# Weight staging as single jobs given out by an account of engine times, and x kept as seven fp32 pieces

## The chip, the core and the metric

One core of one Trainium2 chip runs the kernel. Time is device time in microseconds, from runs of the whole program. PE is TensorE (matmuls, into PSUM), DVE is VectorE, ACT is ScalarE, POOL is GpSimd, SP is the engine that only issues DMAs here; each works through its own queue in order. ACT issues a few DMAs too.

## The reference

Attention without softmax, a norm, and two gated networks, one after the other:

```python
kv = np.einsum('bhsd,bhse->bhde', k, v)            # 8 batches, 8 heads, 576 tokens, 64 wide
out = np.einsum('bhsd,bhde->bhse', q, kv)
rms = np.sqrt(np.mean(out * out, axis=-1, keepdims=True) + 1e-06)
x = (out / rms * g_norm)                           # then 4608 tokens x 512
gate = 1.0 / (1.0 + np.exp(-(x @ w_gate)))         # first network, 512 -> 1536 -> 512
x = gate * (x @ w_val) @ w_out
g = x @ w_gate2                                    # second network, same sizes
silu = g * (1.0 / (1.0 + np.exp(-g)))
y = silu * (x @ w_val2) @ w_out2
```

The weights arrive as float64.

## The kernel before

**Tiling.** The 4608 tokens are nine blocks j of 512. Each network's 1536 columns are twelve slices of 128, and a phase (the list `PH`) walks all nine blocks with six of them: phases 0 and 1 are the first network, 2 and 3 the second. A phase's half of the output goes to DRAM (`pd`) and is added to in the next one. A matmul in full fp32 precision is three in the fast format fp32r: every operand is split into a high part (a copy that rounds, on ACT) and a low part (source minus high part, on DVE or POOL), and low x high, high x low and high x high are summed in one PSUM bank.

**Seven products.** Phase 0 multiplies plainly (`gv_plain`, units of one slice). In phases 1 to 3 a unit is two slices and runs Winograd's form of the 2x2 block product (`gv_win`): seven products of 12 matmuls in place of eight, in the order 11, T2, T1, T3, 21, 22, T4 of x. For that x comes in seven pieces of 128 x 512, namely three quarters of the block and four differences of quarters, each with high and low part, 14 in all; the weights come in seven pieces too. Behind a unit's seven products stand the output products of the unit before (`parts_of(tail)`, `finish`).

**x of the first network.** The attention leaves x in DRAM (`xd`). In phase 1 `x_steps` loads four quarters per block into `xl` buffers, forms the differences and both parts, and writes them into one of two sets of x tiles, one to the right (`x`), one to the left (in `arena`), in turn.

**x of the second network.** When a block of phase 1 is done, `comp_steps` splits its seven pieces and stores the 14 parts to DRAM (`xc`), through two places of `spare` in turn, and for the last block through two `raw` buffers (`xz`). In phases 2 and 3 there is one set of x tiles: `x_load` stands behind each product of a block's last unit and loads the next block's piece, both parts, 512 KB, into the place that this product was the last to read.

**Weights.** `rounded` makes fp32 out of a float64 chunk by six steps (`o1` on ACT, `o3` to `o6` on DVE, `o7` on DVE or POOL). Phase 0's own weights are rounded directly into place (`put_direct`). For the later phases `stage` and `stage_pair` load a chunk into `raw`, round it, form the sums, split them and store them to DRAM (`wd`); `place`, `place_most` and `place_seven` load them from there shortly before use. 72 chunks of 128 x 512 are rounded in all.

**What sets the order.** The program is written in the order of PE's work; ACT, DVE and POOL keep the order of writing nearly everywhere, while SP's DMAs are ordered by a scheduler from their readiness. Between products `tick` advances the count `now` and lets queues of thunks (`att`, `xq`, `kq`, `wq`, `pq`, `rq`) run at a pace that meets their due times; `budget` limits how many DVE and POOL steps one tick may emit. Phase 1's weights are in `pq`, those of phases 2 and 3 in `rq`, as fixed lists of steps:

```python
    def pace(self, dt, pairs=False):
        rate = dt * max(((i + 1) / max(1, z[0] - now[0]) for i, z in enumerate(self.items[self.at:])), default=0.0)
        self.credit = min(self.credit + rate, 1.0 + rate)
        n = int(self.credit)
        self.credit -= n
        self.run(n, True, pairs)
```

## Time and profile before

| | us |
|---|---|
| median of 3 runs (lowest, highest) | 1775.51 (1774.17, 1776.54) |
| the profiled execution | 1774.87 |
| its span, from the first to the last instruction | 1773.1 |

Granted TensorE clock over the span: 0.995 of full speed. Busy time by stretch, in us, and the busy share of the 16 DMA engines:

| stretch | about | PE | DVE | ACT | POOL | DMA |
|---|---|---|---|---|---|---|
| 100 to 545 | phase 0 | 444.37 | 245.83 | 162.15 | 205.99 | 0.63 |
| 545 to 958 | phase 1 | 412.63 | 336.84 | 177.44 | 260.86 | 0.64 |
| 958 to 1367 | phase 2 | 402.32 | 276.17 | 154.45 | 217.50 | 0.57 |
| 1367 to 1773 | phase 3 | 401.37 | 232.34 | 126.03 | 170.14 | 0.43 |

Matmuls overlap one another and their ends are modelled, so a busy PE can still lose time between them; how far apart equal pieces of its work start tells more than its busy share.

### The profile page before, as it was taken

The numbers are of one execution on the slowest core, as the hardware profiler recorded it, in microseconds if no ns is written. First come the engines' busy times: TensorE is split into PE (matmuls) and PEld (weight loads), VectorE is DVE, ScalarE is ACT, GpSimd is POOL, SyncE is SP. The second block draws the span as 40 slices with busy tenths as digits, with TensorE's granted clock in tenths as the row PEclk, the third lists the DMA queues.
The fourth block names the chain that finished last, engine by engine and source line by source line (L and its number), as shares of the span: only waits on it lengthen the run. The fifth ranks groups of instructions, "written<-read, shape, count | busy, mean of one in ns | idle before, by whom it ended". The sixth has DMA issues, their size and how long they took to land.

```text
span 1773.1 us, 33796 instructions
## 1 busy us (share of the span) xinstructions
PE 1745.6 (98%) x12844; PEld 1629.4 (92%) x12844; DVE 1160.1 (65%) x1853; ACT 677.6 (38%) x1472; POOL 898.2 (51%) x991
## 2 busy tenths in 40 slices
PE   7899999999999999999999999999999999999998
PEld 6788888888889999999999999999999999999998
DVE  5766556554455888988875666767775555555555
ACT  4654233333343444444443333433333333333332
POOL 1654456531254576767662455556563344444444
PEclk8999999999999999999999999999999999999999
DMA  9968796457457455565679834444459743343432
GB/s 290 276 166 229 225 229 158 123 153 244 143 178 281 160 181 194 191 220 176 201 272 353 295 118 165 175 174 164 170 185 331 245 132 131 131 132 131 132 131 72
DMA packets 282467, 339.39 MB, mean 191 GB/s; under 512 B 96192, under 2 KB 205376, under 8 KB 282048
## 3 DMA queue, kind: packets, MB, share of 16 engines
q1 hardware_dynamic: 267136, 324.11, 56.4%
q10 hardware_dynamic: 15168, 13.11, 2.5%
q8 instruction: 101, 1.65, 0.4%
q14 instruction: 62, 0.51, 0.1%
HBM read 217.09 MB, written 120.06 MB: 190 GB/s over the span
## 4 chain that ended last, share of the span: by engine, by line
PE 91%; DMA 4%; POOL 2%; DVE 1%; issue 1%; ACT 0%; SPq 0%; DVEq 0%; POOLq 0%; ACTq 0%
PE gv L795 42%; PE gv L717 16%; PE o L928 14%; PE o L907 8%; PE o L893 8%; PE ops L222 1%; DMA vm<-in_v_dram 1%; PE kvps L172 1%; DMA x<-xc 1%; DMA raw<-in_moe_w_out_dram 1%; DMA xc<-xz 0%; PE xTp L269 0%; DMA pl<-pd 0%; DMA xd<-xT 0%; POOL he L837 0%
## 5 line engine op out<-in xcount | busy, mean ns | idle before, releaser
L795 PE MATMUL gv<-x,wgv 128*128 128x256 f32 x5796 | 694.3, 280 | 7.0 <-DMA x<-xc 3.2
L795 PEld LDWEIGHTS gv<-x,wgv 128*128 128x128 f32 x5796 | 685.9, 188 | 10.3 <-ACT u L803 2.3
L717 PE MATMUL gv<-x,wgv 128*128 128x512 f32 x1296 | 315.4, 394 | 3.1 <-ACT x L276 2.3
L717 PEld LDWEIGHTS gv<-x,wgv 128*128 128x128 f32 x1296 | 241.4, 189 | 53.7 <-ACT x L276 2.8
L342 DVE TENSOR_TENSOR u<-u,gv 128x512 f32<-128x512 f32 x162 | 110.1, 680 | 83.0 <-PE gv L795 79.2
L893 PE MATMUL o<-h,wo 128*128 128x512 f32 x648 | 161.4, 393 | 0.0
L893 PEld LDWEIGHTS o<-h,wo 128*128 128x128 f32 x648 | 120.1, 188 | 24.2 <-issue 0.3
L768 ACT ACTIVATE w<-v 128x256 f32<-128x256 f32 x81 | 33.9, 418 | 235.4 <-DVE v L342 224.8
L795 PEld LDWEIGHTS gv<-arena,wgv 128*128 128x128 f32 x1008 | 119.5, 188 | 1.3 <-DVE v L342 0.2
L795 PE MATMUL gv<-arena,wgv 128*128 128x256 f32 x1008 | 119.9, 279 | 0.0
L725 DVE TENSOR_TENSOR sg<-sg,gv 128x512 f32<-128x512 f32 x54 | 36.9, 683 | 102.1 <-PE gv L717 99.5
L907 PE MATMUL o<-h,arena 128*128 128x512 f32 x432 | 101.5, 390 | 0.0
L837 POOL TENSOR_TENSOR spare<-w,spare 128x256 fp32r<-128x256 f32 x54 | 42.6, 788 | 112.6 <-ACT spare L836 112.5
L421 POOL TENSOR_TENSOR u<-u,s 128x512 f32<-128x512 f32 x36 | 49.6, 1377 | 97.9 <-DVE s L418 85.8
L837 POOL TENSOR_TENSOR he<-w,he 128x256 fp32r<-128x256 f32 x54 | 41.8, 775 | 109.1 <-ACT he L836 109.1
L907 PEld LDWEIGHTS o<-h,arena 128*128 128x128 f32 x432 | 79.8, 188 | 15.9
L407 DVE TENSOR_SCALAR u<-u 128x512 uint32<-128x512 uint32 x72 | 48.1, 668 | 65.3 <-ACT u L403 65.0
L342 DVE TENSOR_TENSOR v<-g,gv 128x512 f32<-128x512 f32 x81 | 55.7, 687 | 53.0 <-PE gv L795 32.9
L928 PE MATMUL o<-arena,h 128*128 128x256 f32 x636 | 83.0, 279 | 0.0
L837 POOL TENSOR_TENSOR spare<-g,spare 128x256 fp32r<-128x256 f32 x54 | 49.3, 932 | 66.3 <-ACT spare L836 66.3
L928 PE MATMUL o<-arena,he 128*128 128x256 f32 x648 | 81.5, 279 | 0.0
L928 PE MATMUL o<-arena,spare 128*128 128x256 f32 x648 | 81.5, 279 | 0.0
(155 smaller groups left out, 3030.8 us busy)
## 6 DMA issues: line engine op xcount, KB each, us to landing
x<-xc SPq DMA_DIRECT2D x126, 512.0 KB, 5.3
wgv<-wd SPq DMA_DIRECT2D x72, 448.0 KB, 7.5
xc<-spare SPq DMA_DIRECT2D x112, 256.0 KB, 3.3
pl<-pd SPq DMA_DIRECT2D x80, 256.0 KB, 4.3
wd<-raw SPq DMA_DIRECT2D x72, 256.0 KB, 2.3
raw<-in_moe_w_gate_dram SPq DMA_DIRECT2D x24, 512.0 KB, 5.2
raw<-in_moe_w_val_dram SPq DMA_DIRECT2D x24, 512.0 KB, 4.4
raw<-in_moe_w_out_dram SPq DMA_DIRECT2D x24, 512.0 KB, 4.7
```

The source lines that it names most:

```text
L172: nc.tensor.matmul(kvps[b][e * D:(e + 1) * D, hp, :D], lt, rt, start=(r == hp == 0), stop=(r == R and hp == NP - 1), skip_group_check=True)
L342: nc.vector.tensor_tensor(out=out, in0=a, in1=b, op=ALU.add)
L407: nc.vector.tensor_scalar(ub, ub, 3, None, op0=ALU.logical_shift_left)
L421: (E_O7 if eng is not nc.vector else eng).tensor_tensor(out=st["u"], in0=st["u"], in1=st["s"], op=ALU.add)
L717: nc.tensor.matmul(ps, w[:, e, a, kk, :], x[b][:, kk, :], start=(n == 0), stop=(n == 3 * KD - 1))
L725: nc.vector.tensor_tensor(out=sg, in0=sg, in1=bank[1], op=ALU.mult)
L768: nc.scalar.activation(o, t[:, 0], AF.Silu if f else AF.Sigmoid)
L795: nc.tensor.matmul(ps[:, e], w[:, l, kk], xs[x_at(r)[0]][:, x_at(r)[1], kk], start=(fresh and e == n == kk == 0), stop=(not more and e == ...
L837: nc.gpsimd.tensor_tensor(out=hs[z][:, 1], in0=x, in1=hs[z][:, 0].bitcast(F32), op=ALU.subtract)
L893: nc.tensor.matmul(ps, l, r, start=(fresh and t == 0), stop=(last and t == 2))
L907: nc.tensor.matmul(ps, l, r, start=(fresh and e == t == 0), stop=(last and e == 1 and t == 2))
L928: nc.tensor.matmul(ps[:, t], h[:, r, cs], w[:, Ax[a] + 7 * l], start=(start and t == n_ == 0), stop=(stop and t == 1 and n_ == 2), skip_gr ...
```

## The change

Three things change, and the matmuls stay.

**Jobs.** `stage` and `stage_pair` go. `group_jobs` cuts the staging of a pair of slices into single jobs: a load, each step of a rounding, each sum, copy, subtraction and store. A job names the engines that may do it with a time for each, and the buffers it touches. An account holds the time of PE's work so far (`clock`, advanced by `passed` behind each product) and when each engine will be free (`free`, advanced by `use` beside every instruction of the kernel and by `moved` for DMAs). `pump` gives out the job that can start soonest on an engine whose backlog stays under `HORIZON`, as long as more jobs remain than `LINE_` allows at this point. Where DVE or POOL can do a job, the account chooses.

**x in seven fp32 pieces.** `seven_steps` makes the four differences of the first network's x in phase 0 (for blocks 0 to 2 from a second reading) and stores them (`x7`, three quarters stay in `xd`); `comp_steps` stores the second network's seven pieces as they are, the differences made in place behind the store of what they overwrite. `x_load` now serves phases 1 to 3 and loads one fp32 piece, 256 KB, into the place of the low part; `run_splits` then puts a copy (high part) at 4.2 us and a subtraction in place (low part) at 5.2 us behind the load, by the account. One set of x tiles is left.

**Buffers.** The left set of x tiles goes; in its room stands `stage`, with buffers for two more groups of jobs in phase 1 (sides B and C), and later `arena`, which holds the output weights of phases 2 and 3 together with the new `wob`. In phase 0 there are buffers in the room of the x tiles (side R, `aside`) and of the attention (side T). Staging now ends in phase 1 (`ASIDE_END`).

```diff
+    def use(e, share=1.0):
+        free[e] = max(free[e], clock[0]) + share * WORK[e]
+    def sooner(k):
+        c = clock[0]
+        e = "V" if max(free["V"], c) + 0.85 <= max(free["G"], c) + 1.4 + FAVOR[k] else "G"
+        use(e)
+        return e
+    def moved(mb):
+        free["D"] = max(free["D"], clock[0]) + mb / 0.39
+    def passed(n, cols):
+        clock[0] += n * (0.117 if cols == HB else 0.228)
...
-        late["arena"] = shifted(late["L"], 11 * KB, F32R, ARENA_AT, "arena")
+        late["wob"] = shifted(late["L"], 4 * KB, F32R, ARENA_AT, "wob")
         late["spare"] = late["L"].tile([P, 8, HB], F32R, name="spare")
+        late["stage"] = shifted(late["L"], 7 * KB, U32, W7_AT, "stage", "ar")
...
+    def pump():
...
+        while len(jobs) > floor:
+            held_keys, best = set(), None
+            for n, z in enumerate(jobs[:WINDOW]):
+                keys = z.keys | old_of(z) | ({(side_of(z), z.new[0])} if z.new else set())
+                if not keys & held_keys:
+                    r = max((ready.get(k, 0.0) for k in keys), default=0.0)
+                    for e, d in z.does.items():
...
+                        t = max(clock[0], free[e])
+                        start = max(t, r)
+                        d = shared(e, d, start)
+                        if start <= t + BUBBLE[e] and start + d <= clock[0] + HORIZON[e] * short - soon.get(e, 0.0):
+                            best = min(best or (9e9,), (round(max(start - t, 0.0) / STEP) + (start + d) / 100 * (len(z.does) > 1), n, e, start))
+                held_keys |= keys
+            if not best:
+                return
+            emit(jobs[best[1]], best[2], best[3])
...
     def x_load(ph, j, b):
         k, i = x_at(b)
-        t = x_tiles(ph, j)[k][:, i:i + 2].rearrange("p c k a -> p (c k a)").bitcast(F32)
-        nc.sync.dma_start(out=t, in_=xc[j][:, 2 * b * DM:2 * (b + 1) * DM])
+        h, l = [x_tiles(ph, j)[k][:, i + e] for e in range(2)]
+        if PH[ph][0]:
+            nc.sync.dma_start(out=l.rearrange("p k a -> p (k a)").bitcast(F32), in_=xc[j][:, b * DM:(b + 1) * DM])
+        elif b > 2:
+            nc.sync.dma_start(out=l.rearrange("p k a -> p (k a)").bitcast(F32), in_=x7[j][:, (b - 3) * DM:(b - 2) * DM])
...
+        def hi():
+            nc.scalar.activation(h, l.bitcast(F32), AF.Copy)
+            use("A")
+        def lo():
+            ENG[sooner(0)].tensor_tensor(out=l, in0=l.bitcast(F32), in1=h.bitcast(F32), op=ALU.subtract)
+        splits.extend(((clock[0] + LANDED, hi), (clock[0] + LANDED + 1.0, lo)))
...
+    def run_splits():
+        while splits and splits[0][0] <= clock[0]:
+            splits.pop(0)[1]()
...
-        return [H(0, 0, 0), W(0, 0, 0), D((0, 0), (0, 1), (0, 0)), H(1, 1, 2), W(1, 1, 2), D((0, 1), (1, 1), (0, 1)), H(0, 0, 3), W(0, 0, 3, po), nop, D((0, 0), (1, 1), (0, 0)),
-                H(0, 1, 5), W(0, 1, 5, po), nop, H(1, 0, 1), W(1, 0, 1), D((1, 0), (1, 0), (0, 0)), H(0, 0, 4), W(0, 0, 4, po), nop, H(1, 0, 6), W(1, 0, 6, po)]
+            return lambda: ENG[sooner(1)].tensor_tensor(out=st[o], in0=st[a], in1=st[b], op=ALU.subtract)
+        return [store(0, 0, 0), store(1, 1, 2), store(1, 0, 1), nop, nop, D((0, 0), (0, 1), (0, 0)), nop, store(0, 0, 3), D((0, 1), (1, 1), (0, 1)), nop, store(0, 1, 5),
+                nop, nop, D((0, 0), (1, 1), (0, 0)), nop, store(0, 0, 4), D((1, 0), (1, 0), (0, 0)), nop, store(1, 0, 6)]
...
+    def between():
+        run_splits()
+        if "L" in late and now[0] >= tick_of(*ASIDE_END):
+            drain("B", "C")
+        if wq.at >= n_direct[0] and not -5 <= now[0] - tick_of(1, 0, 0) < 13 and not HOLD[0] <= now[0] - tick_of(2, 0, 0) < HOLD[1]:
+            pump()
...
     def tick(dt=1.0, room=9, pool=1):
         now[0] += dt
+        run_splits()
...
-        if not first and not -5 <= now[0] - tick_of(1, 0, 0) < 13:
-            if pq.at < len(pq.items):
-                pq.pace(dt)
-            else:
-                rq.pace(dt, HOLD <= now[0] - tick_of(2, 0, 0) < 42)
+        between()
```

**ACT in the first unit of phase 2's second block.** Here `he`, `hl`, `v` and `w` belong to the unit before, `xz` is a split piece of the second network's last block, and `u<-gv` is the copy of the new unit's first product. Before:

```order
L768 ACTIVATE v<-g 128x256
L836 ACTIVATE he<-w 128x256
L682 ACTIVATE xz<-pl 128x512
L768 ACTIVATE w<-u 128x256
L682 ACTIVATE xz<-pl 128x512
L836 ACTIVATE he<-g 128x256 x2
L836 ACTIVATE he<-w 128x256
L803 ACTIVATE u<-gv 128x512
L836 ACTIVATE hl<-v 128x256
```

The same place in the changed kernel, where `x_4990` to `x_4992` are the three tiles of x:

```order
L970 ACTIVATE v<-g 128x256
L1044 ACTIVATE he<-w 128x256
L819 ACTIVATE x_4991<-x_4991 128x512
L819 ACTIVATE x_4992<-x_4992 128x512
L970 ACTIVATE w<-u 128x256
L819 ACTIVATE x_4990<-x_4990 128x512 x2
L1044 ACTIVATE he<-g 128x256 x2
L1044 ACTIVATE he<-w 128x256
L1010 ACTIVATE u<-gv 128x512
```

The two `xz` copies left their places, and copies of loaded x pieces stand there.

**SP at the change to the last block of phase 2** (`wd` is staged weights, `xc` the second network's x, `pd` the half outputs, `wgv` phase 3's weights). Before:

```order
L605 DMA x_9024<-xc_10108 128x1024
L605 DMA x_9025<-xc_10108 128x1024
L469 DMA wd_11_465<-raw 128x256
L605 DMA x_9025<-xc_10108 128x1024
L605 DMA x_9026<-xc_10108 128x1024
L469 DMA wd_11_465<-raw 128x512 x2
L605 DMA x_9024<-xc_10108 128x1024 x2
L469 DMA wd_11_465<-raw 128x512
L469 DMA wd_11_465<-s 128x512
L469 DMA wd_11_465<-u 128x512
L469 DMA wd_11_465<-s 128x512
L605 DMA x_9026<-xc_10108 128x1024
```

After:

```order
L1182 DMA pd_6_13730<-yg 128x2x256
L1182 DMA pd_6_13730<-yu 128x2x256
L810 DMA x_4990<-xc_10125 128x512
L810 DMA x_4991<-xc_10125 128x512 x2
L810 DMA x_4992<-xc_10125 128x512
L810 DMA x_4990<-xc_10125 128x512 x2
L810 DMA x_4992<-xc_10125 128x512
L773 DMA wgv_6_14444<-wd_6_460 128x896 x3
```

The stores of staged weights have left the stretch, and each x load has half the columns.

**SP at the turn from phase 2 to phase 3** (`arena<-wd` is phase 3's output weights). Before:

```order
L572 DMA wgv_8_14850<-wd_8_462 128x896 x4
L605 DMA x_9024<-xc_5910 128x1024
L605 DMA x_9025<-xc_5910 128x1024 x2
L572 DMA wgv_9_14871<-wd_9_463 128x896 x4
L605 DMA x_9026<-xc_5910 128x1024
L594 DMA arena<-wd_7_461 128x256 x2
L594 DMA arena<-wd_7_461 128x768 x2
L605 DMA x_9024<-xc_5910 128x1024 x2
L605 DMA x_9026<-xc_5910 128x1024
```

After:

```order
L773 DMA wgv_8_14696<-wd_8_462 128x896 x4
L810 DMA x_4990<-xc_5994 128x512
L810 DMA x_4991<-xc_5994 128x512
L773 DMA wgv_9_14717<-wd_9_463 128x896
L810 DMA x_4991<-xc_5994 128x512
L773 DMA wgv_9_14717<-wd_9_463 128x896 x3
L810 DMA x_4992<-xc_5994 128x512
L798 DMA arena<-wd_7_461 128x256 x2
L798 DMA arena<-wd_7_461 128x768 x2
L810 DMA x_4990<-xc_5994 128x512 x2
L810 DMA x_4992<-xc_5994 128x512
```

The weights stand around x as before, one of them now between the second and the third piece, and x's loads are half as large.

## Rows read from the trace of the kernel before

**Rows 1.** The page's first part: busy time, share of the span, instructions.

```profile
PE 1745.6 (98%) x12844; PEld 1629.4 (92%) x12844; DVE 1160.1 (65%) x1853; ACT 677.6 (38%) x1472; POOL 898.2 (51%) x991
```

**Rows 2.** Stretches: length, busy PE, PEld, DVE, ACT, POOL (instructions), clock, DMA, GB/s.

```profile
100.00:545.00 445.00, 444.37 (x2375) 370.02 (x2373) 245.83 (x370) 162.15 (x291) 205.99 (x264) 1.00 0.63 178
545.00:958.00 413.00, 412.63 (x2915) 386.07 (x2915) 336.84 (x485) 177.44 (x356) 260.86 (x200) 1.00 0.64 221
...
545.00:560.00 15.00, 15.00 (x111) 14.18 (x111) 4.96 (x10) 4.96 (x10) 0.00 (x0) 1.00 0.98 355
```

**Rows 3.** The chain in order of time, phase 1: start us, us, what.

```profile
574.82 9.80 PE gv L795 x84
...
605.37 9.80 PE gv L795 x84
...
666.46 9.80 PE gv L795 x84
...
942.66 9.80 PE gv L795 x84
```

**Rows 4.** The chain, phase 2 and the first block of phase 3.

```profile
973.20 5.62 PE gv L795 x48
...
1013.53 8.48 PE o L928 x72
...
1057.83 8.40 PE o L928 x72
1066.23 9.80 PE gv L795 x84
...
1101.96 8.40 PE o L928 x72
...
1234.34 8.47 PE o L928 x72
...
1278.99 8.54 PE o L928 x72
...
1324.72 8.40 PE o L928 x72
...
1372.64 8.40 PE o L928 x72
```

**Rows 5.** Timeline, phase 2's second block: start us, us, what [idle before, releaser].

```profile
1005.32 0.63 ACT L682 ACTIVATE xz<-pl 128x512 fp32r<-128x512 f32 x1 [4.22 <-DMA xc<-xz]
...
1006.77 0.57 ACT L803 ACTIVATE u<-gv 128x512 f32<-128x512 f32 x1
...
1007.40 3.07 PE L795 MATMUL gv<-x,wgv 128*128 128x256 f32 x24 [1.21 <-ACT u L803]
```

**Rows 6.** The chain: two loads of x, from issue to landing.

```profile
1315.32 7.62 DMA x<-xc
...
1357.94 7.87 DMA x<-xc
```

**Rows 7.** Timeline, SP at the change to phase 2's last block.

```profile
1314.67 0.32 SPq L469 DMA_DIRECT2D wd<-s  x1
```

**Rows 8.** Splits of x by line, whole span: duration ns min/median/max, first, last start.

```profile
L656 ACT ACTIVATE x<-xl x35: 614/618/635, 507.3 to 906.4; 128x512 fp32r<-128x512 f32 x35
...
L659 POOL TENSOR_TENSOR x<-xl,x x20: 1281/1302/1755, 520.4 to 909.2; 128x512 fp32r<-128x512 f32 x20
...
L659 DVE TENSOR_TENSOR x<-xl,x x15: 682/841/1828, 510.7 to 903.1; 128x512 fp32r<-128x512 f32 x15
```

**Rows 9.** X loads of 512 KB between 1380 and 1700 us.

```profile
DMA to landing us min/median/max: 3.4/5.0/6.8
```

**Rows 10.** DMA issues, 1400 to 1700 us: KB each, median us to landing.

```profile
pl<-pd SPq DMA_DIRECT2D x32, 256.0 KB, 3.5
```

**Rows 11.** DMA issues, 1340 to 1375 us.

```profile
x<-xc SPq DMA_DIRECT2D x7, 512.0 KB, 7.9
```

**Rows 12.** Timeline, the first unit of phase 3.

```profile
1365.94 4.59 PE L795 MATMUL gv<-x,wgv 128*128 128x256 f32 x24 [1.98 <-DMA x<-xc]
```

More of the change, by code (lines that the diff above doesn't have):

```diff
@@ new lines, in sides, with side_of, drain @@
+    def sides():
+        if "L" in late:
+            return ("B", "C") if now[0] < tick_of(*ASIDE_TO) else ()
+        return ("R",) if "R" in late and clock[0] < ASIDE[0] else ()
+    def side_of(z):
+        if z.group.side is None:
+            for k in sides():
+                if not any(y.group.side == k for y in jobs):
+                    return k
+            return "A"
+        return z.group.side
+    def drain(*which):
+        while any(z.group.side in which for z in jobs):
+            z = next(z for z in jobs if z.group.side in which)
+            emit(z, next(iter(z.does)), clock[0])
@@ new lines, in shared, with emit @@
+    def shared(e, d, start):
+        if e == "V":
+            return d + min(SHARE[0], max(0.0, free["G"] - start))
+        if e == "G":
+            return d + min(SHARE[1], max(0.0, free["V"] - start))
+        return d
+    def emit(z, e, start):
+        keys = z.keys | old_of(z)
+        jobs.remove(z)
+        z.group.side = side_of(z)
+        if z.new:
+            rings.setdefault((z.group.side, z.new[0]), []).append(z.new[1])
+        if e == "D":
+            z.f()
+            moved(z.does["D"])
+            end = max(clock[0] + 2.0, free["D"]) + LATE
+        else:
+            (z.f(e) if len(z.does) > 1 else z.f())
+            start = max(start, clock[0])
+            end = start + shared(e, z.does[e], start)
+            free[e] = max(free[e], end)
+            end += 0.1
+        for k in keys:
+            ready[k] = end
@@ new lines, in T_tile, with begin_small @@
+    def T_tile(t, n):
+        x = aside["T"][t if t != "u" else f"u{n}"]
+        return x.bitcast(U32).rearrange("p (a b) -> p a b", b=2) if t == "raw" else x
+    def begin_small():
+        if "R" in late or wq.at < n_direct[0] or any(z.group.side == "T" for z in jobs) or now[0] >= tick_of(*T_TO):
+            return
+        fresh = []
+        for z in jobs:
+            if z.group.side is None and z.group not in fresh:
+                fresh.append(z.group)
+        if len(fresh) < 2:
+            return
+        if "T" not in aside:
+            t = {"raw": at.tile([P, DM, 2], U32, tag="raw", name="raw").rearrange("p a b -> p (a b)"), "u0": at.tile([P, DM], F32, tag="u", name="u")}
+            t["u1"], t["s"], t["sg0"], t["sg1"] = [wk.tile([P, NB], F32, tag="sn", bufs=4, name=n) for n in ("us", "ss", "sg", "sg")]
+            aside["T"] = t
+        g = fresh[1]
+        k = next(i for i, z in enumerate(jobs) if z.group is g)
+        n = sum(z.group is g for z in jobs)
+        jobs[k:k + n] = group_jobs(*g.of, True)
@@ L680, in run, with S, store @@
+                moved(0.25)
+            return run
+        def S(i, n):
+            def run():
+                hi, lo = [t[:, 2 * i:2 * i + 2, n * HB:(n + 1) * HB] for t in x_tiles(0, j)]
+                split(hi, lo, st[i, n])
+            return run if use_ else nop
+        def D(o, a, b):
+            return lambda: sub(st[o], st[a], st[b])
+        def store(i, n, o):
             def run():
-                z[o] = buf()
-                nc.scalar.activation(z[o][:, :2], st[i, n], AF.Copy)
@@ L739, in h_places @@
             hw["n"] = 0
-        if p == 2 and first:
-            while not rq.whole():
-                rq.run(1)
-            hw["far"] = [wk.tile([P, 2, HB], F32R, tag=t, name="hl") for t in "usu"]
-        elif p == 2 and len(hw["L"]) == 2:
+        if p == 2 and len(hw["L"]) == 2:
             hw["L"].append([wk.tile([P, 2, HB], F32R, tag="xl", bufs=3, name="hl") for _ in range(3)])
@@ L1123, in evac @@
             if i == 1:
-                ring = [0]
-                def buf():
-                    if j == NBLK - 1:
-                        return wk.tile([P, 4, HB], F32R, tag="raw", name="xz")
-                    ring[0] ^= 4
-                    return late["spare"][:, ring[0]:ring[0] + 4]
-                while j == NBLK - 1 and not rq.whole():
-                    rq.run(1)
-                th = comp_steps(j, {divmod(z, 2): part.pop((ph, j, z)) for z in range(4)}, buf)
+                th = comp_steps(j, {divmod(z, 2): part.pop((ph, j, z)) for z in range(4)})
                 for k, z in enumerate(th):
@@ L1358, in attention_two_ffn @@
                 first = (ph, j) == (1, 0)
[L1359 to L1361 removed]
+                if not queued and (i > 1 or j > 0) and ph == 0 and (nxt[0] == 0 or "R" in late):
                     queued = True
```

446 lines of the change are left out of this document (277 added, 169 removed).

## The prediction

> **What bounds the kernel now.** I read the page first. The matmuls cover 98% of the span [rows 1], so the time is the list of matmuls plus what TensorE loses between them. The change leaves the list alone: on PE's queue both programs hold 12336 matmuls of the same shapes, in the same order but for 88 of them in phase 0, where whole groups change place. So I only ask where TensorE stands still. The stretches by phase come next: from 100 us on the granted clock is 1.00, the upper of TensorE's two levels (2.4 GHz), and phase 0 and phase 1 are covered to within 0.6 us of PE time [rows 2]. "Covered" hides short holes, since a matmul's end is modelled, so I took the chain of waits as a clock: the same piece of work stands there once a unit or once a block, and a distance that is too long is a loss.
>
> Phase 1: four undisturbed units take 666.46 - 605.37 = 61.09, or 15.27 each. The 24 units from 574.82 to 942.66 take 367.84 where 366.54 are due: 1.30 lost [rows 3].
>
> Phases 2 and 3: the last output products of a block (72 matmuls) recur every 1101.96 - 1057.83 = 44.13 us where nothing disturbs. Before that, 1013.53 to 1057.83 is 44.30 (0.17 lost); 1234.34 to 1278.99 is 44.65 (0.52); 1278.99 to 1324.72 is 45.73 (1.60); 1324.72 to 1372.64, in which phase 2 turns into phase 3, is 47.92 (3.79). From a block's second unit to those products it is 1101.96 - 1066.23 = 35.73; across the turn from phase 1 to phase 2 it is 1013.53 - 973.20 = 40.33 (4.60) [rows 4]. After 1372.64 nothing is lost.
>
> The sum is 1.30 + 4.60 + 0.17 + 0.52 + 1.60 + 3.79 = 12.0 us. That is nearly all that a change of staging can win. What is lost in the first 100 us belongs to the attention and the first weights; the orders are the same there on all queues until about 145 us.
>
> **The change part by part.**
>
> *x of the second network, compressed (turn from phase 1 to phase 2).* Before, the last block's x is cut into high and low halves in two `xz` buffers, and ScalarE may write the next one only after a store has landed. It stands in order: at 1005.32 it has idled 4.22 us for such a store, and behind it wait the `he` copies and the copy `u<-gv` that PE needs at 1007.40 [rows 5]. The changed kernel has no `xz`: the fp32 piece is stored as it is, and ScalarE's row there holds only copies of x pieces whose loads left a unit earlier. What goes is 4.60. What is late next: VectorE or GpSimd now overwrite a piece only after its store has landed, which holds up the next stores but nobody on PE's path, since those pieces are read a phase later. Between 0 and 4.60 left; I take 0.4, near the low end, because the row names the cause and it is gone.
>
> *No staging in phase 2.* Of the 72 roundings of a weight chunk, 44 stand before phase 1, 16 in it and 12 in phase 2. In the changed order it is 47, 25 and 0. So SP's queue in phase 2 holds no weight stores between the x loads. The last x load of a block leaves only at 1315.32, when the weight stores ahead of it on the queue have left, the last of them at 1314.67; it lands 7.62 us later, and PE waits [rows 6, 7]. The losses 0.17, 0.52 and 1.60 should go: left between 0 and 2.29, taken 0.3.
>
> *x as seven fp32 pieces, split in place.* Each of the 126 loads shrinks from 512 to 256 KB, and 63 stores of 256 KB go as well. Added are, per block of phases 1 to 3, seven copies on ScalarE (0.62 us each) and seven subtractions, 155 of 189 of them on VectorE (0.68 alone, 1.83 at worst) and the rest on GpSimd (1.28 to 1.76) [rows 8]. They are new on the path: a piece can only be loaded after its product in the block's last unit, and must be split before the same product of the next block. The room: seven products 9.80 plus the 24 output matmuls (8.40 / 3 = 2.80) less the product's own 9.80 / 7 = 1.40 is 11.2 us in phases 2 and 3, and 15.27 - 1.40 = 13.9 in phase 1 [rows 3, 4]. Landing takes 3.4 to 6.8 us for 512 KB in the quiet part [rows 9] and 3.5 for a 256 KB load there [rows 10]. The account books 4.2 until the copy. So a quiet change needs 4.2 + 0.62 + 0.68 to 1.83 = 5.5 to 6.7 of 11.2, and even 6.8 + 2.45 = 9.3 fits. Cost 0; the cover is the 2 to 5 us of slack, and if it is gone each us of lateness is a us per block.
>
> *The turn from phase 2 to phase 3* is not quiet: the next phase's weights fill the queues, and x takes 7.9 us at the median [rows 11]. PE stands 1.98 us for a piece issued at 1357.94 that landed 7.87 later [rows 6, 12]. It is the fifth of seven. At 355 GB/s, the rate of a full stretch [rows 2], half a piece is 0.74 us, so five halves bring it 3.7 us forward; its split costs 0.62 + 0.68 to 1.83 = 1.3 to 2.45. Left of the 1.98: nothing to 0.7. All 3.79 could stay; I take 0.6.
> The Trainium skill (DMA: Bandwidth & Descriptors, Bandwidth) speaks against counting half the bytes as half the time: its table has 64 KB at 0.95 us and 1 MB at 6.15. An estimate on the line between them makes 256 KB 0.59 of 512 KB. By that the five pieces come 3.0 forward, 0.6 us more is left, and the forecast would be 1767.4; no run so far shows both sizes in one full queue.
>
> *x of the first network from DRAM, and single jobs.* Phase 0 gets the 36 differences of x (0.68 to 1.83 on VectorE, as above), 36 stores and 12 more loads; in return phase 1 loses them and the 56 copies and 56 subtractions that made the pieces of the second network's x, and gets 25 roundings for 16. By the orders' counts times the durations above, no engine comes over 90% of any 25 us from 100 us on, before or after. In phase 0 the cover is that h is used a unit (445 / 54 = 8 us) after it is made. PE has 0.6 us to gain there, and loses at most what phase 1, with VectorE busy 337 of 413 us, loses now (1.3): taken 0.5. Phase 1: between 0 and twice today's 1.30, taken 1.0. At the turn from phase 0 to 1 PE loses nothing now though the queues are full (0.98) [rows 2]; the new order puts four raw loads of 512 KB into it, on which ScalarE waits ahead of a unit's first copy. Between 0 and 2 (four loads at 355 GB/s are 5.9 us, less the 4.2, three products, from the first product's end to the need of that copy), taken 0.5.
>
> **The sum.** Left or new: 0.4 + 0.3 + 0.6 + 0.5 + 1.0 + 0.5 = 3.3. Won: 12.0 - 3.3 = 8.7. The profiled execution took 1774.87 (span 1773.1), so 1766.2; the median of the runs lies 0.64 above it: **1766.8**.
>
> **The rivals.**
> *B, the queues decide.* The losses at 1315 and 1357 are late transfers; if place loads of weights, not staging and not x's size, set them, 1.60 and 3.79 stay. For it: the same `wgv` and `arena` loads stand around x in the new order. Against it: 1315 lies ahead of them. Time: 1766.8 + 1.5 + 3.2 = 1771.5.
> *C, staging comes back as small holes.* The account is a guess at engine times; where it is wrong jobs bunch, in the worst case at a drain, and a gate or a copy is late. Price: a hole like the 0.52 of one block [rows 4] in every block of phases 0 and 1 is 18 x 0.52 = 9.4, of which 1.5 is counted: 1774.7. If the account does nothing of what it says, this is what is seen. Against it: the orders show no burst beyond 5.5 us of work on one engine.
> *D, slower: splits too late.* One mechanism at one place: at each of the 18 block changes of phases 2 and 3 the subtraction ends after its product is due. It decides from a landing of 11.2 - 2.45 = 8.8 us; the jammed median is 7.9 [rows 11]. ScalarE's wait for a late load also holds the copy that the next unit needs. At 1.0 us per change, half of the 1.98 that one late piece costs now [rows 12], it is +18: 1784.8.
> The Trainium skill (SBUF — State Buffer, Who interferes with whom) would feed this: a VectorE operation with two SBUF inputs and a GpSimd one that reads SBUF lock each other out for a whole instruction. The spread 682 to 1828 ns of the same subtraction agrees.
>
> **How the numbers follow.** Forecast 0.58, B 0.16, C 0.18, D 0.08. A measurement tells 0.2%, 3.6 us: faster is below 1772.0, slower above 1779.1. Faster: 0.57 of the forecast, 0.09 of B, 0.04 of C: 0.70. Slower: 0.07 of D, 0.01 of C: 0.08. Same: 0.22. The range: all 12.0 and phase 0's 0.6 won, and nothing new, is 1763; C at its price is 1775; that leaves out D and the worse half of C, 0.17.
>
> **What would show it.** After the change the chain should show blocks of 44.1 from 973 to the end but for one at the turn to phase 3 of at most 45; no ScalarE wait for a store of `xc`; x at 256 KB landing in 3 to 4 us in the quiet part; ScalarE copies of x that wait under 1 us for their load. Wrong would be: PE waits named after the subtraction of x at most changes (D), blocks still 47.9 at the turn (B), or units of phase 1 over 15.5 (C).

## The result: 1.3% slower

The changed kernel takes 1798.03 us at the median (1796.44 to 1802.5), the kernel before 1775.37 us in the same comparison: a ratio of 1.0132, with a 95% interval from 1.0112 to 1.0151. The profiled execution has a span of 1800.7 us, 27.6 more than before.

The page of the changed kernel shows TensorE as covered as before; only the two groups of the seven products take longer (line 1001 after, line 795 before; "busy, mean ns of one"), 282 and 191 ns against 280 and 188:

```profile
PE 1768.0 (98%) x12844; PEld 1646.1 (91%) x12844; DVE 1221.9 (68%) x1947; ACT 707.4 (39%) x1535; POOL 886.4 (49%) x960
...
L1001 PE MATMUL gv<-x,wgv 128*128 128x256 f32 x6804 | 827.9, 282 | 3.3 <-ACT u L1010 1.6
L1001 PEld LDWEIGHTS gv<-x,wgv 128*128 128x128 f32 x6804 | 820.4, 191 | 6.3 <-ACT u L1010 1.8
```

The stretches answer to [rows 2] (length, then busy PE, PEld, DVE, ACT, POOL with instructions, granted clock, DMA share, GB/s). In the changed kernel the part of phase 0 up to 545 us has 8.9 us in which PE isn't covered, all between 350 and 500 us:

```profile
100.00:545.00 445.00, 436.14 (x2308) 358.14 (x2307) 291.20 (x410) 162.71 (x296) 226.17 (x273) 0.99 0.74 217
545.00:958.00 413.00, 413.00 (x2847) 385.27 (x2846) 308.76 (x470) 162.10 (x323) 248.31 (x200) 1.00 0.63 219
...
350.00:400.00 50.00, 47.42 (x209) 38.03 (x208) 38.12 (x52) 15.34 (x29) 29.50 (x34) 1.00 0.59 178
400.00:450.00 50.00, 47.42 (x197) 37.26 (x197) 30.85 (x41) 17.97 (x33) 19.66 (x16) 0.97 0.89 289
450.00:500.00 50.00, 46.30 (x192) 36.41 (x191) 34.45 (x45) 19.61 (x37) 27.39 (x25) 0.97 0.70 242
```

The kernel before has no such hole there, and a third less VectorE work:

```profile
350.00:400.00 50.00, 50.00 (x227) 41.54 (x226) 25.39 (x42) 16.80 (x30) 19.34 (x25) 1.00 0.58 155
400.00:450.00 50.00, 50.00 (x222) 41.44 (x221) 20.88 (x31) 15.68 (x28) 9.64 (x10) 1.00 0.70 234
450.00:500.00 50.00, 50.00 (x223) 41.40 (x222) 22.91 (x32) 17.63 (x32) 21.19 (x20) 1.00 0.46 146
```

The other loss shows where nothing stands at all. From 1420 to 1740 us PE is covered without a hole and every matmul has 256 columns; only their number in the 320 us differs. The kernel before fits 2744 in, one every 116.6 ns:

```profile
1420.00:1740.00 320.00, 320.00 (x2744) 320.00 (x2743) 186.27 (x335) 100.41 (x266) 137.91 (x168) 1.00 0.41 132
```

The changed kernel fits 2703 in, one every 118.4 ns, at the same granted clock of 1.00:

```profile
1420.00:1740.00 320.00, 320.00 (x2703) 320.00 (x2702) 221.39 (x373) 124.72 (x316) 147.93 (x170) 1.00 0.31 92
```

With the start of every matmul in the two traces the account closes. A stand is here what an interval between two starts has above 117 ns (256 columns) or 227 ns (512), if it is over 145 or 290; the rest is pace. Phase 0 ends where the first product of phase 1 starts.

| us | before | changed | difference |
|---|---|---|---|
| start of phase 1 | 549.6 | 565.7 | +16.1 |
| pace of phases 1, 2, 3 | 407.0 + 393.8 + 406.2 | 414.1 + 399.6 + 412.2 | +18.9 |
| stands in phases 1, 2, 3 | 1.2 + 6.6 + 3.8 | 0.0 + 1.3 + 2.9 | -7.4 |
| sum | | | +27.6 |

So most of the stands of phases 1 to 3 went, as was predicted: 4.2 of 11.6 us are left. Not all of that is the new order's doing, since a slower pace hides stands too: in the run b_near below, which alters only places, they fall to 7.2. What PE still waits for in the changed kernel is three short waits (engine, line, what it waited for; us in total, times, longest):

```profile
PE gv L1001 <- ACT u L1010: 1.6, 1, 1.6
PE gv L1001 <- POOL x L823: 1.0, 1, 1.0
PE gv L1001 <- DVE v L377: 0.7, 1, 0.7
```

The time went to two things that the prediction had at nothing or next to it: the pace of the seven products, and phase 0.

### The profile page after: what moved, and what is told of

Read it like the earlier page. It is cut to its first block, busy times and chain, and to the rows that moved or that the text cites. A ratio compares the mean times of both kernels' runs of the same rounds, so it can differ in the third digit from the quotient of the medians.

```text
span 1800.7 us, 33917 instructions
## 1 busy us (share of the span) xinstructions
PE 1768.0 (98%) x12844; PEld 1646.1 (91%) x12844; DVE 1221.9 (68%) x1947; ACT 707.4 (39%) x1535; POOL 886.4 (49%) x960
## 4 chain that ended last, share of the span: by engine, by line
PE 85%; DMA 5%; DVE 4%; POOL 2%; issue 2%; ACT 2%; SPq 1%; ACTq 0%; DVEq 0%; POOLq 0%
PE gv L1001 44%; PE o L1141 14%; PE gv L920 11%; PE o L1119 8%; PE o L1104 6%; PE ops L230 1%; DMA x<-xc 1%; DMA raw<-in_moe_w_out_dram 1%; PE kvps L178 1%; DMA xl<-xd 1%; DMA qm<-in_q_dram 0%; DVE xl L373 0%; DMA aside<-in_moe_w_gate_dram 0%; DMA aside<-in_moe_w_val_dram 0%; POOL aside L651 0%
## 5 line engine op out<-in xcount | busy, mean ns | idle before, releaser
L1001 PE MATMUL gv<-x,wgv 128*128 128x256 f32 x6804 | 827.9, 282 | 3.3 <-ACT u L1010 1.6
L1001 PEld LDWEIGHTS gv<-x,wgv 128*128 128x128 f32 x6804 | 820.4, 191 | 6.3 <-ACT u L1010 1.8
L920 PEld LDWEIGHTS gv<-x,wgv 128*128 128x128 f32 x1296 | 240.9, 189 | 57.7 <-DVE sg L930 4.2
L823 DVE TENSOR_TENSOR x<-x 128x512 fp32r<-128x512 f32 x155 | 147.2, 970 | 45.2 <-ACT x L819 41.3
L819 ACT ACTIVATE x<-x 128x512 fp32r<-128x512 f32 x189 | 113.6, 620 | 29.7 <-DMA x<-xc 11.7
L1119 PE MATMUL o<-h,wob 128*128 128x512 f32 x432 | 102.1, 392 | 0.0
L1045 POOL TENSOR_TENSOR he<-g,he 128x256 fp32r<-128x256 f32 x54 | 50.7, 958 | 92.2 <-ACT he L1044 82.4
L1119 PEld LDWEIGHTS o<-h,wob 128*128 128x128 f32 x432 | 79.8, 188 | 16.6
L1010 ACT ACTIVATE u<-gv 128x512 f32<-128x512 f32 x81 | 48.3, 597 | 110.5 <-PE gv L1001 107.5
L395 ACT ACTIVATE h<-sg 128x512 fp32r<-128x512 f32 x54 | 34.0, 630 | 116.3 <-DVE sg L930 111.5
L1141 PEld LDWEIGHTS o<-arena,h 128*128 128x128 f32 x636 | 78.0, 188 | 0.0
```

What stands on the lines that cost most here:

```text
L395: nc.scalar.activation(hi, src, AF.Copy)
L819: nc.scalar.activation(h, l.bitcast(F32), AF.Copy)
L823: ENG[sooner(0)].tensor_tensor(out=l, in0=l.bitcast(F32), in1=h.bitcast(F32), op=ALU.subtract)
L920: nc.tensor.matmul(ps, w[:, e, a, kk, :], x[b][:, kk, :], start=(n == 0), stop=(n == 3 * KD - 1))
L1001: nc.tensor.matmul(ps[:, e], w[:, l, kk], xs[x_at(r)[0]][:, x_at(r)[1], kk], start=(fresh and e == n == kk == 0), stop=(not more and e == ...
L1010: nc.scalar.activation(u, c1, AF.Copy)
```

## The experiments

### The pace: where x lies against the weights

Nothing stands between these matmuls, so what changed must lie in the matmul itself. The built programs give each tile a place in SBUF. All parts of `wgv` that phases 1 to 3 read begin at 64 modulo 128 bytes, in both kernels. In the kernel before, x begins at 96. In the changed kernel the buffers `aside` take the places of x0 and x1 early, the tiles lie in another order, and x0 and x1, ten of the fourteen parts, begin at 64 like the weights; x2 stays at 96. Theory A: the place of x against that of the weights sets the pace. The first two runs were written with modulo 64 in mind.

```diff
-aside["x"] = [late["R"].tile([P, ...], F32R, tag=f"x{i}", ...) for i in range(3)]
+aside["x"] = [shifted(late["R"], ..., F32R, (0, (8 if i == 1 else 0)), ...) for i in range(3)]
```

(and the same for `aside`; 8 columns are 32 bytes behind x1, which moves x1 and x0 down)

> The changed kernel with one thing altered: 32 bytes are left free behind the tile x1, so that x1 and, under it, x0 begin at 32 modulo 64 instead of at 0 modulo 64, where the weights wgv begin too; no instruction is added or moved. In the trace of the changed kernel a 256-column matmul of phases 1 to 3 that reads x0 or x1 starts 119.5 to 120.2 ns after the one before it, and in that of the kernel before, where x began at 32 modulo 64, 116.7 to 118.3 ns. Theory A (the place of x against the place of the weights sets the pace): the mean interval of the 6804 matmuls falls from 119.4 to about 117.0 ns, 6804 x 2.4 = 16 us less, 1798 - 16 = 1782 us (range 1779 to 1786). Rival (the pace comes from something else that runs beside the matmuls, such as the new DMA or the splits): intervals stay at 119 to 120 ns, 1795 to 1801 us.

> The control for the 32-byte shift: 64 bytes are left free behind x1, so x0 and x1 move, but begin at 0 modulo 64 again. Theory A (place modulo 64 against the weights): nothing changes, 119.4 ns and 1795 to 1801 us. If instead any move of x out of its place helps, it is as fast as the run with 32 bytes, 1782 us.

Measured: 1788.86 us with 32 bytes (ratio to before 1.0075, 1.0056 to 1.0095), and 1775.69 with the 64 bytes of the control (1.0002, 0.9990 to 1.0013). So theory A fell in its form: the control, which should have done nothing, was the better one. From 1420 to 1740 us the control shows

```profile
1420.00:1740.00 320.00, 320.00 (x2759) 320.00 (x2758) 224.62 (x378) 123.94 (x315) 153.91 (x176) 1.00 0.32 93
```

with the same work on VectorE as in the changed kernel (224.62 and 221.39), so neither that work nor the DMA makes the 118.4 ns. What fits is the distance from the weights to x modulo 128: 0 in the changed kernel, 96 with 32 bytes, 64 in the control. The next runs turned this on the kernel before, with its own program and only places altered (bytes left free behind x2 and a `wo` tile), and on the distance that x had there:

> The kernel before, with nothing altered but places: 32 bytes left free behind x2 and 96 behind the second wo tile of the right side, so that x0, x1 and x2 of the right side begin at 64 modulo 128, where all weights wgv begin; the x in the arena stays at 96. The two runs that moved x in the changed kernel gave 120.1 ns between two 256-column matmuls with x1 at the same place modulo 128 as wgv, 118.3 ns with 32 bytes between the places, 114.5 ns with 64. Theory A2 (the distance between the places of x and wgv modulo 128 sets the pace: 0 slow, 32 or 96 middle, 64 fast): the 5711 matmuls of before that read these tiles go from 117.4 to about 119.9 ns, 5711 x 2.5 = 14 us more, 1790 us (range 1786 to 1793). Rival (the pace in the changed kernel came from its other traffic, and the moves there acted through the place of its staging buffers): 1774 to 1778 us.

> The kernel before with 96 bytes left free behind x2 and 32 behind the second wo tile, so that x0, x1 and x2 of the right side begin at 0 modulo 128, 64 bytes off the places of wgv. Theory A2: 5711 matmuls go from 117.4 to about 114.8 ns, 5711 x 2.6 = 15 us less, 1761 us (range 1758 to 1765), with no instruction altered. Rival: 1774 to 1778 us.

> The changed kernel with 96 bytes left free behind x1, so that x0 and x1 begin at 96 modulo 128 as x does in the kernel before, 32 bytes above the places of wgv; nothing else is altered. So far the distance from wgv to x modulo 128 gave these mean intervals of 256-column matmuls: 0: 119.7, 119.7 ns (two builds); 32: 116.8 to 118.2; 64: 114.8 to 116.3; 96: 118.2 ns. Theory A2 (the distance sets the pace): about 116.9 ns for the 4843 matmuls that read x0 or x1, 2.8 ns less than in the changed kernel, and some tenths for x2, 14 us less: 1784 us (range 1781 to 1787), which is what the change costs with x at the distance of the kernel before. Rival (only 64 bytes' distance helps, because x0 and x1 then also move against the other buffers): as with 32 bytes, 1787 to 1791 us.

Measured: distance 0 makes the kernel before slow, 1792.04 us (1.0086, 1.0071 to 1.0101), by its pace alone (1207.0 us of pace become 1226.9, the stands shrink):

```profile
1420.00:1740.00 320.00, 320.00 (x2689) 320.00 (x2688) 182.91 (x327) 99.48 (x264) 132.83 (x162) 1.00 0.40 128
```

Distance 64 did not make it fast: 1775.28 us (0.9995, 0.9986 to 1.0004). And the changed kernel with x at the distance of before, modulo 128, took 1789.56 us (1.0076, 1.0061 to 1.0091), not 1784. These builds together, with the mean interval after a matmul that reads x, by the distance modulo 128 (intervals over 150 ns left out; in b_near and b_far the x in `arena`, which wasn't moved, is left out):

| kernel | distance of x0, x1 / x2 | mean ns, x0 and x1 | matmuls, 1420 to 1740 | median us |
|---|---|---|---|---|
| before | 32 / 32 | 116.8 (all x) | 2744 | 1775.4 |
| before, b_near | 0 / 0 | 119.7 (x0, x1, x2) | 2689 | 1792.0 |
| before, b_far | 64 / 64 | 116.1 (x0, x1, x2) | 2742 | 1775.3 |
| changed | 0 / 32 | 119.7 | 2703 | 1798.0 |
| changed, e_line8 | 96 / 32 | 118.2 | 2723 | 1788.9 |
| changed, e_line24 | 32 / 32 | 117.9 (all x) | 2722 | 1789.6 |
| changed, e_line16 | 64 / 32 | 114.8 | 2759 | 1775.7 |
| changed, f_x2 (below) | 64 / 64 | 116.3 (all x) | 2745 | 1782.1 |

What is shown: the places alone, with no instruction altered, move the changed kernel by 22.3 us (1798.03 to 1775.69) and the kernel before by 15.4 (1776.66 to 1792.04 in the same comparison). Distance 0 is the slowest in both. What isn't shown is a rule for the others: modulo 128, the same distance gives 116.8 ns in one kernel and 117.9 in the other, 64 gives 114.8 or 116.3, and moving x2 as well (f_x2) brought 116.3, not the 114.6 expected.

Part of that scatter may come from counting modulo 128. Counted modulo 256, the places in all seventeen programs sort the means better:

| distance modulo 256 | mean ns |
|---|---|
| 0 and 128 | 119.5 to 119.8 |
| 96 | 119.6 to 119.7 |
| 160 | 117.4; 118.2 (x0, x1 of e_line24) |
| 224 | 118.2 |
| 32 | 116.7 to 117.2 in fourteen programs; 118.2 (x2 of the changed kernel and of e_late6) |
| 64 | 116.4 to 116.8 |
| 192 | 114.8 to 115.9 |

So e_line24 did not put x where it lay before: there x0 and x1 are 160 bytes off, while x in the kernel before is 32 off. Of the 18.9 us of pace, e_line24 gives back 10.4 (1225.9 to 1215.5). For the other 8.5 an estimate from this table is that 32 bytes would bring 5 to 7 more (4860 matmuls at 118.2 ns, against 116.8 to 117.1). This sorting was made after the runs, no run tested it, and the two values of 118.2 at 32 bytes don't fit it.

The control also shows what the change is worth without the accident of places. e_line16 loses 13.4 us in phase 0 against the kernel before; it wins 8.9 of pace and 5.3 of stands behind it, and so comes out level.

### Phase 0: chunks whose loads have not landed

In the changed kernel PE waits mostly for h there, and ScalarE for loads:

```profile
PE o L1104 <- ACT h L395: 5.2, 3, 2.1
PE gv L920 <- DVE sg L930: 2.6, 3, 1.3
...
ACT aside L444 <- DMA aside<-in_moe_w_val_dram: 10.5, 2, 9.7
...
ACT u L444 <- DMA raw<-in_moe_w_gate_dram: 5.9, 3, 4.0
ACT aside L444 <- DMA aside<-in_moe_w_out_dram: 5.8, 2, 3.7
```

The timeline of the longest of these (start, length, what [idle before, releaser]) shows how a load becomes a stand of PE:

```profile
406.95 0.60 ACT L928 ACTIVATE sg<-gv 128x512 f32<-128x512 f32 x1 [0.33 <-PE gv L920]
417.28 0.66 ACT L444 ACTIVATE aside<-aside 128x512 f32<-128x512 f32 x1 [9.73 <-DMA aside<-in_moe_w_val_dram]
...
417.97 0.43 DVE L449 TENSOR_SCALAR aside<-aside 128x512 uint32<-128x512 uint32 x1 [10.54 <-ACT aside L444]
...
423.51 1.40 DVE L459 TENSOR_SCALAR aside<-aside 128x512 uint32<-128x512 uint32 x1
...
426.55 1.33 DVE L459 TENSOR_SCALAR s<-u 128x512 uint32<-128x512 uint32 x1
427.80 0.68 DVE L930 TENSOR_TENSOR sg<-sg,gv 128x512 f32<-128x512 f32 x1
...
428.50 0.63 ACT L395 ACTIVATE h<-sg 128x512 fp32r<-128x512 f32 x1 [4.41 <-DVE sg L930]
...
429.19 1.52 PE L1104 MATMUL o<-h,wo 128*128 128x512 f32 x2 [2.10 <-ACT h L395]
```

ScalarE stands 9.73 us before the first step of a chunk whose load the account took for landed 2.0 us after the transfer's end by its own reckoning. VectorE, whose next instruction is that chunk's second step, stands 10.54 us with it. Both then work off a row of staging steps, and the gating `sg` and the copy of h come behind them. This stand of 2 us costs more than itself: the granted clock of the next 4 us is near the lower level (1.2 GHz):

```profile
427.00:429.00 2.00, 0.09 (x1) 0.00 (x0) 1.47 (x2) 0.50 (x1) 1.84 (x3) 1.00 1.07 356
429.00:431.00 2.00, 1.81 (x4) 1.13 (x5) 1.83 (x2) 0.44 (x2) 2.00 (x3) 0.57 0.81 244
431.00:433.00 2.00, 2.00 (x7) 1.57 (x6) 1.40 (x2) 1.00 (x2) 1.73 (x2) 0.58 0.92 266
```

The Trainium skill (TensorE: Matmul & The Clock Gate, Architectural detail) has ScalarE and VectorE as strict first-in-first-out queues; the 9.73 and 10.54 us agree. In the program, 16 chunks are started between fp32r matmuls 1200 and 1800 (about 380 to 520 us), 10 in the kernel before. Theory B: the 2.0 us are too short. Rival: the engines or the DMA are full there.

```diff
-end = max(clock[0] + 2.0, free["D"]) + LATE
+end = max(clock[0] + 2.0, free["D"]) + (LATE if "L" in late else EARLY)    # EARLY = 6.0
```

> The changed kernel, with the account's delay for a transfer (LATE) raised from 2.0 to 6.0 us until the last attention step (phase 0); x stays where it is. From 350 to 500 us of the trace of the changed kernel TensorE loses about 16 us against the kernel before, part of it standing, part of it at the lower clock level after a stand. Theory B (ScalarE stands at the head of its queue before the first step of a staged chunk whose load was given 2.0 us but landed 5 to 10 us after its issue, and the split of h queues behind it): ScalarE's waits for raw and aside (29 us in that stretch) fall below 10 us, TensorE's waits for h fall from 8 us to under 2 us, and 8 to 14 us come back: 1784 to 1790 us. Rival (the DMA engines are full there, or VectorE is, so that the same wait only moves to another place): 1794 to 1801 us.

> Both alterations at once, 32 bytes behind x1 and 6.0 us for a transfer in phase 0. If the two losses are the whole of the slowdown and independent of each other, they add: 1798 - 16 - 11 = 1771 us (range 1766 to 1776), about what was predicted for the change. If one of them hides the other, no better than the better of the two alone, 1780 us or more.

Measured: 1807.47 and 1799.80 us, worse than without it in both pairs. Yet the place it was made for did as theory B says: ScalarE's waits for `raw` and `aside` between 345 and 545 us fall from 32.5 to 7.8 us, and from 350 to 500 us PE has no hole. But 12 chunks are started there now, not 16, so this run alone doesn't tell the delay from the number:

```profile
350.00:400.00 50.00, 50.00 (x234) 41.87 (x233) 35.75 (x50) 18.81 (x34) 28.91 (x36) 1.00 0.74 227
400.00:450.00 50.00, 50.00 (x222) 41.40 (x222) 34.16 (x44) 17.14 (x32) 22.85 (x19) 1.00 0.82 262
450.00:500.00 50.00, 50.00 (x222) 41.41 (x221) 32.77 (x47) 18.08 (x33) 15.80 (x12) 1.00 0.66 223
```

So VectorE and DMA are not full there: 102.7 us of VectorE work go in where 103.4 made holes. But the new order meets something else earlier. At 280 us PE now stands 7.21 us, behind the same pattern with another load, that of x for its split, ahead of `sg`; with smaller stands before it, all of phase 0's loss now arises between 245 and 295 us (13.7 us), and none behind that:

```profile
278.77 0.63 ACT L395 ACTIVATE x<-xl 128x512 fp32r<-128x512 f32 x1 [9.71 <-DMA xl<-xd]
279.31 0.65 ACT L444 ACTIVATE u<-raw 128x512 f32<-128x512 f32 x1
279.86 0.57 ACT L928 ACTIVATE sg<-gv 128x512 f32<-128x512 f32 x1
...
280.49 3.78 PE L920 MATMUL gv<-x,wgv 128*128 128x512 f32 x8 [7.21 <-ACT sg L928]
```

and phase 2 grew from 400.8 to 409.1 us. The following runs have 64 bytes behind x1 (e_line16) and try fewer or later chunks near 400 us alone: 6.0 us from the opening of the right side only (f_r6; f_x2 with x2 moved too), the same to the end of the program (h_rl6; h_rl6f with a flatter line too), and flatter lines, which say how many jobs may be left at a given time:

```diff
-LINE_ = (((0, 2, 0), (1, 0, 0), 780, 300), ((1, 0, 0), (1, 8, 0), 400, 0))
+LINE_ = (((0, 2, 0), (1, 0, 0), 780, 460), ((1, 0, 0), (2, 4, 0), 460, 0))    # g_line
+LINE_ = (((0, 2, 0), (1, 0, 0), 780, 420), ((1, 0, 0), (1, 8, 0), 420, 0))    # g_line2
```

> The changed kernel with 64 bytes behind x1 (1775.7 us by itself) and the account's 6.0 us for a transfer, now only from the opening of the right side (about 350 us) to the end of phase 0, so that the new stand at 257 to 285 us, which the 6.0 us in all of phase 0 brought, does not come. Theory B (ScalarE's waits for raw and aside at the head of its queue cost phase 0 its time): phase 1 begins at about 550 us as in the kernel before, not at 563, 12 to 13 us less: 1764 us (range 1760 to 1768). Rival (what is given out later in phase 0 is missing later, at the turns of phases 1 and 2, where the run with 6.0 us in all of phase 0 stood some 7 us more): 1769 to 1774 us.

> As the run with 64 bytes and 6.0 us on the right side only, and with 96 bytes behind x2 and 32 behind the second wo tile, so that x2 too begins 64 bytes off the places of wgv. Theory A2: its 1864 matmuls go from 117.4 to about 114.6 ns, 1864 x 2.8 = 5 us less than that run, about 1759 us (range 1755 to 1764). Rival (x2 already stands well): no difference from that run.

> The changed kernel with 64 bytes behind x1 (1775.7 us by itself, of which phase 0 is about 13 us longer than in the kernel before) and a flatter line for the account: 460 jobs instead of 300 may be left when phase 1 begins, and none when block 4 of phase 2 begins instead of block 8 of phase 1. Between matmuls 1200 and 1800 (about 380 to 520 us) the program then starts 10 chunks, as the kernel before does, and not 16; the staging ends in phase 2, as in the kernel before. Theory V (too many chunks are started in the last 150 us of phase 0; each one's first step on ScalarE stands on its load): phase 1 begins at 550 to 554 us and not at 563, and nothing comes back later: 1765 us (range 1761 to 1769). Rival R (it is the waits on single landings, however few chunks there are, and they go where the chunks go): 1771 to 1778 us.

> The changed kernel with 64 bytes behind x1 and a line between the two: 420 jobs may be left when phase 1 begins (300 in the changed kernel, 460 in the flat line), and all is staged by block 8 of phase 1 as in the changed kernel. Between matmuls 1200 and 1800 the program starts 12 chunks (16 in the changed kernel, 10 with the flat line). Theory V for phase 0: phase 1 begins at 553 to 557 us instead of 563, and phase 2, with hardly any staging left in it, doesn't stand 11 us as with the flat line: 1766 to 1770 us, faster than both kernels. Rival R (a chunk that isn't started in phase 0 costs as much where it goes): 1774 to 1779 us, with stands at the end of phase 1.

> The changed kernel with 64 bytes behind x1 and 6.0 us for a transfer from the opening of the right side to the end of the program; the line is the changed kernel's. The run with 6.0 us to the end of phase 0 only (1776.2 us) stood 8 us at the end of phase 1, 4.1 us of it with TensorE behind a copy of ScalarE that stood behind the first step of a chunk not yet landed. Theory B (the account's 2.0 us, wherever it is used, lets ScalarE stand): these stands fall to 2 or 3 us, 1770 us (range 1767 to 1773). Rival V (the chunks are too many for the time, and the loss moves with them): 1775 us or more, with stands at the end of phase 1 or in phase 2.

> As the run before it, with a flatter line (380 jobs left at the start of phase 1, none at block 4 of phase 2): 14 chunks between matmuls 1200 and 1800, and staging into phase 2 as in the kernel before. Theory B: few stands in any phase, 1766 to 1770 us, faster than both kernels. Rival V: the loss shows in phase 2, as with the flat line alone (11 us there), 1775 to 1780 us.

Measured, with the starts of the phases from the profiled executions:

| run | phase 1 begins | phase 1 | phase 2 | phase 3 begins | median us |
|---|---|---|---|---|---|
| e_line16 | 563.0 | 403.8 | 393.7 | 1360.5 | 1775.7 |
| f_r6 | 556.6 | 412.7 | 393.5 | 1362.8 | 1776.2 |
| h_rl6 | 555.9 | 410.8 | 400.1 | 1366.8 | 1779.0 |
| h_rl6f | 556.8 | 405.9 | 403.5 | 1366.2 | 1776.1 |
| g_line | 552.6 | 405.6 | 406.9 | 1365.1 | 1779.1 |
| g_line2 | 559.2 | 420.2 | 394.8 | 1374.1 | 1784.8 |

Every one wins in phase 0, the flat line 10.4 us, and every one gives it back at the next place. With the flat line PE's waits from 950 to 1260 us are mostly for ScalarE's first copy in phase 2:

```profile
PE gv L1001 <- ACT u L1010: 8.0, 5, 3.0
```

With the line in between, ScalarE stands 12.2 us near the end of phase 1 for one load:

```profile
ACT u L444 <- DMA raw<-in_moe_w_val_dram: 12.2, 1, 12.2
```

With 6.0 us from the right side on (h_rl6), where theory B expected 2 or 3 us of stands in phase 1, 8.2 remain, now mostly for sums on VectorE, and PE waits 3.9 us for a split of x as phase 2 begins:

```profile
PE gv L1001 <- POOL x L823: 3.9, 1, 3.9
PE gv L1001 <- DVE u L377: 2.8, 2, 1.9
PE gv L1001 <- DVE v L377: 2.5, 3, 1.0
```

So theory B does not cover the cost: the rival that the loss moves with the chunks held in all of these runs. Two more took the buffers of the right side away:

```diff
-WINDOW, ASIDE, HORIZON = 100, [385], {"A": 1.6, "V": 1.7, "G": 3.5}
+WINDOW, ASIDE, HORIZON = 100, [0], {"A": 1.6, "V": 1.7, "G": 3.5}
```

> The changed kernel with 64 bytes behind x1 and no staging in the buffers of the right side (the aside tiles that stand where x0 and x1 will be); the line stays. Between matmuls 1200 and 1800 12 chunks are started, not 16. If the second set of buffers is what lets ScalarE and SyncE run into waits, phase 1 begins at 550 to 553 us: 1764 us; theory V gives a part of that, 555 to 558 us and 1768 to 1771 us; if neither counts, 1774 to 1778 us.

> Both: no buffers of the right side and the flatter line; 10 chunks between matmuls 1200 and 1800, all in the one set of buffers that the kernel before has. Theory V and the theory of the second set agree: phase 1 begins at 550 to 553 us, 1762 to 1766 us. If the loss of phase 0 remains (557 us or later), it comes from the seven pieces of x and their loads and stores, not from the staging.

Measured: 1802.38 and 1794.65 us. These two compare badly, since without `aside` the tiles change order again: x0 and x1, and with them a third of the weights, come to lie elsewhere. Where the distance is 96 bytes modulo 128, the pace is 118.4 ns. Beside e_line8, which has that distance for x0 and x1, phase 1 begins at 557.7 and 551.3 us, not 565.2, and phase 3 at 1384.1 and 1375.4, not 1371.8. With one set of buffers and the flat line phase 0 is thus nearly what it was before the change; the seven pieces of x cost it little more than the holes between 365 and 385 us, which all these runs show but the two with 6.0 us in all of phase 0.

g_noRl also shows that a late load alone makes no hole. ScalarE stands 11.49 us there, longer than the 9.73 of the changed kernel, and from 385 to 520 us PE waits 0.2 us in all; VectorE's `sg` follows 4 us behind:

```profile
427.91 0.66 ACT L444 ACTIVATE u<-raw 128x512 f32<-128x512 f32 x1 [11.49 <-DMA raw<-in_moe_w_val_dram]
...
431.89 0.68 DVE L930 TENSOR_TENSOR sg<-sg,gv 128x512 f32<-128x512 f32 x1
```

In the changed kernel VectorE works off eight staging steps, 6.1 us, from 421.73 us on before its `sg` at 427.80. What PE loses between about 390 and 520 us, against the kernel before, goes with the chunks started there:

| chunks | runs | loss, us |
|---|---|---|
| 16 | changed, e_line8, e_line16, e_line24 | 10.2 to 12.5 |
| 14 | f_r6, f_x2, h_rl6, h_rl6f (6.0 us) | 2.7 to 5.5 |
| 12 | g_noR, g_line2 (2.0 us) | 4.8, 6.5 |
| 12 | e_late6, e_both (6.0 us) | 0.0, 0.2 |
| 10 | g_line, g_noRl (2.0 us) | 0.0, 0.5 |

So the holes come of both, late loads and the staging steps queued behind them. ScalarE waits 30.4 us for chunks in this stretch of g_noRl and 32.4 in the changed kernel, but with 10 chunks that costs 0.5 us and with 16 it costs 12.5. With 12 chunks the later first step takes the loss away, with 14 it doesn't. How the two share the loss no run separates, since places, buffers and order differ between these programs too. No run is faster than the kernel before: the best are level with it.

## Why the prediction was wrong

**The pace: the step that failed first.** The prediction said that the change leaves the list of matmuls alone and asked only where TensorE stands still. The list is the same, the places of its operands are not, and the order of the tiles, which sets them, was never looked at. This term stood at 0 and measured +18.9 us; places alone move the pace by 10.4 us (e_line24) to 27.8 (e_line16, 1225.9 to 1198.1), but that all 18.9 come from them isn't shown. The Trainium skill (SBUF — State Buffer, Who interferes with whom) gives TensorE two independent read ports, for the moving operand and for the weights, and says that it never waits on anyone. By that, places would cost nothing; b_near disagrees, with 2689 matmuls instead of 2744 by places alone.

**Phase 0: a term mis-sized, 0.5 for +16.1.** Its bounds (-0.6 to 1.3) came from busy time, at most 90% in any 25 us. That was right (VectorE reaches 90% at its worst in phase 0) and beside the point. The price lies in the order of the queues: ScalarE's wait of 9.73 us for a landing, and the staging steps that VectorE then works off ahead of `sg`. The prediction named this at the turn from phase 0 to 1 ("raw loads on which ScalarE waits ahead of a unit's first copy", 0 to 2), where nothing was lost; the same pattern 100 us earlier was left out, although the cover it named there, h used 8 us after it is made, is shorter than that wait.

**The turn from phase 1 to 2:** 0.4 left predicted, 1.15 measured, for a split of x on GpSimd. The 4.22 us of ScalarE [rows 5] went, but at 981 us it stands 6.21 us for a load of x, and the splits behind that came late. **Blocks of phase 2:** 0.3 predicted, 0.1 measured. **Phase 1:** 1.0 predicted, 0.0 measured.

**The turn from 2 to 3:** 0.6 predicted, 2.65 measured (1.81 + 0.84). The larger one is a wait for ScalarE's first copy, which stood behind two copies of x that waited 2.34 and 2.80 us for their loads. The halved pieces land in 5.7 us at the median where 7.9 stood [rows 11], a ratio of 0.72; the forecast had counted 0.5. In the quiet part it is 2.8 for 5.0 [rows 9], 0.56, near the 0.59 estimated from the Trainium skill's table (DMA: Bandwidth & Descriptors, Bandwidth). The full queue is worse than either:

```profile
x<-xc SPq DMA_DIRECT2D x7, 256.0 KB, 5.7
```

**x split in place:** predicted free, and free in the quiet parts only. ScalarE's copies of x waited 11.7 us for `xc` in four waits: 6.21 at the turn to phase 2, 2.34 and 2.80 at the turn to phase 3, and 0.34. The sign "under 1 us" thus failed at both turns. **Rivals:** D, slower, was the right side for a wrong reason, so its coming nearest to the time is luck: a split came late at the turn to phase 2, and a copy behind late splits at the turn to phase 3, not at each of 18 changes. C, small holes in phases 0 and 1, is the nearest in mechanism: holes came, in phase 0 only, and most cost more than the 0.52 it was priced at, with the clock falling behind. B is not seen in phase 2.

## To carry to other kernels

When a change alters which tiles are allocated or in which order, compare the places of the matmuls' operands before and after, and count matmuls in a stretch without stands: the count shows a loss that no wait shows. Before a step is put ahead of others on an in-order engine, ask when its load lands in the worst jam, and price the wait together with everything queued behind it, not the engine's busy share. A line that gives work out earlier moves stands as often as it removes them, so the sum over all phases has to be read, not the phase that was mended.

## What the runs showed of the hardware

In a full stretch of 256-column matmuls TensorE's pace goes by the places of x and the weights alone from 118.4 ns (2703 in 320 us) to 116.0 (2759) in the changed kernel, and from 116.6 (2744) to 119.0 (2689) in the kernel before, at the same granted clock; behind matmuls that read x0 or x1 it is 114.8 to 119.7. Weight loads show it too: 191 ns at distance 0 in both kernels, 188 or 189 otherwise. What in the chip does this, the runs don't show; neither does a run settle whether the distance counts modulo 128 or 256. After stands of about 2 us at 427 us the granted clock was 0.57 in the next 2 us and 0.58 in the 2 after, and 1.00 again from 433.
